# A mixer kernel's opening: inverse square root as a power on GpSimd, normalising on GpSimd, first weights from ScalarE's queue, more empty transposes

## The chip, the core and the metric

The kernel runs on one core of one Trainium2 chip. The core has TensorE (matrix products and transposes into PSUM), VectorE, ScalarE, GpSimd and a queue engine, SyncE, that issues most of the transfers. The metric is the time of one execution on the device in microseconds; less is better.

## What is computed

The input x has 2048 rows of 512 numbers. It is normalised along each row, and two branches work on the result: attention with 32 heads of 128 against a window of 512 keys, and a gated block that mixes along the rows. Cut to what matters:

```python
xn = layernorm(x)                                   # 2048 x 512, eps 1e-5
q = (xn @ wq) in 32 heads of 128
p = softmax(q @ k.T * 128**-0.5)                    # 512 keys for each head
s = (p @ v, heads side by side) @ wo
z = gelu(xn @ w_in)                                 # 1376 columns, in two halves of 688
z1, z2 = z[:, :688], layernorm(z[:, 688:])
g = silu((z1 * (w_sp @ z2 + b_sp)) @ w_out)
out = x + s * g
```

## The kernel before

Rows are cut into 16 tiles of 128. Every operand of a product is split into a rounded high part (by ScalarE, L165 and L208) and a low part, the rest (`rest`, L57); each product is three matmuls, high with high, low with high and high with low (`mm3`, L61 to L63). Each engine runs its instructions in the order in which the program writes them; the order is written out by hand, and transfers start in the order of their queue.

The kernel has three stages: attention together with the first half of the gated block's products, then the other half, then the mixing along the rows. This case is about the opening, the first 50 us of the first stage.

The opening brings each tile of x through these steps: load into `sacc` (L174), statistics (`ln_stats`: L181 and L183 on VectorE), inverse square root of the variance (`rsqrt_opening`, L116: one operation on VectorE, a square root on ScalarE, then a reciprocal and a correction in four operations on VectorE), normalising in place (`ln_apply`, L195, VectorE), four transposes on TensorE through PSUM (`ln_flip`, L206), cast to the high part (L208, ScalarE), rest to the low part (L57, VectorE). After that, the tile can go into products: `z1_piece`, twelve matmuls of 344 columns with the first quarter of w_in (the tiles `pT_h` and `pT_l`), whose result goes to memory from ScalarE's queue (L229); and `qproj`, the queries of one head for four tiles at a time.

The operations of an inverse square root are kept in a list, and `tick` puts one of them behind another instruction of VectorE; `finish` puts out what is left of a list before a tile is normalised. One root serves the tiles of one group (`GROUPS`): tiles 0 and 1 alone, 2 and 3 together, then four at a time.

Tiles 0 to 2 have their products in a prologue; each product is cut in the middle, and `start` puts the transposes of the next tile there. Then comes a loop over steps `t` from -7 on. Step `t` transposes tile `t + 11`, takes statistics and normalises for later tiles, makes one piece of the queries, and from `t = 0` on one score block (L259 and L261, softmax), from 12 on products with v, from 17 on the output projection. The list `Z0` says in which steps the products of tiles 3 to 15 with w_in are made.

At the very start TensorE has nothing to multiply, and 24 transposes of the identity into a PSUM tile that nobody reads (`warm`, L355) keep it occupied. SyncE's queue issues the loads in this order: tile 0 of x, first piece of w_in, tile 1, three pieces of w_in, tiles 2 and 3, first piece of the head's weights, tiles 4 to 7, three more pieces, and the rest of x.

Of the kernel before, what the change touches and what calls it, by code (L numbers as in the profile page):

```python
# [17 lines left out]
P = 128  # L18
S, D = 2048, 512
H, DH, W = 32, 128, 512  # L20
NT = S // P
NC = D // P
# [4 lines left out]
EPS = 1e-5  # L27
# [11 lines left out]
def mixer_kernel(ctx: ExitStack, tc: tile.TileContext, x, wh, w_in, w_sp, b_sp, w_out, out):  # L39
# [8 lines left out]
    nc = tc.nc  # L48
# [7 lines left out]
    def rest(engine, lo, whole, hi):  # L56
        engine.tensor_tensor(lo, whole, hi.bitcast(F32), op=OP.subtract)  # L57
# [10 lines left out]
    chains = []  # L68

    def tick(n=1):  # L70

        for _ in range(n):
            for c in list(chains):
                c.pop(0)()
                if not c:
                    chains.remove(c)

    def finish(chain):
        while chain:
            tick()  # L80
# [25 lines left out]
        nc.vector.memset(t[:, :4], 0.5)  # L106
        nc.vector.memset(t[:, 4:], float(0x5F3759DF - (1 << 22) - (1 << 31)))

    def rsqrt_opening(var, y, n, tmp, consts):

        v, r, a = ([tmp[:, k * n:k * n + n] for k in range(3)])
        chain = []
        chains.append(chain)

        def add(f, *args, **kw):
            chain.append(lambda: f(*args, **kw))  # L116

        add(nc.vector.scalar_tensor_tensor, v, var, EPS, consts[:, 8:8 + n], op0=OP.add, op1=OP.mult)
        add(nc.scalar.activation, r, v, AF.Sqrt, scale=-2.0)
        add(nc.vector.reciprocal, r, r)  # L120
        add(nc.vector.tensor_mul, a, r, r)
        add(nc.vector.tensor_mul, a, a, v)
        add(nc.vector.scalar_tensor_tensor, y, a, 1.5, r, op0=OP.add, op1=OP.mult)
        return chain

    stats = ctx.enter_context(tc.tile_pool(name="stats", bufs=2))
    left = ExitStack()
# [11 lines left out]
    sacc = sp.tile([P, NT, D], F32, name="sacc")  # L139
# [5 lines left out]
    def load_piece(key, k):  # L145
        n = 512 if key[0] == "h" else NB
        r = rawp.tile([P, 512], F32, name="raw")
        raw[key, k] = r
        nc.sync.dma_start(r[:, :n], (wh if key[0] == "h" else w_in)[key[1], :, k])

# [4 lines left out]
    def split_piece(key, k, engine):  # L155
        n = 512 if key[0] == "h" else NB
        if key == ("w", 0):
            hi = ap.tile([P, 512], F32R, name="pT_h", bufs=4)
            lo = ap.tile([P, 512], F32R, name="pT_l", bufs=4)
        else:  # L160
            f = FOLLOWS[key][k] if key in FOLLOWS else k
            hi = wp.tile([P, 512], F32R, name=f"wh{f}")
            lo = wp.tile([P, 512], F32R, name=f"wl{f}")
        r = raw.pop((key, k))[:, :n]
        nc.scalar.copy(hi[:, :n], r)  # L165
        rest(engine, lo[:, :n], r, hi[:, :n])
        wt[key, k] = (hi, lo)


    GROUPS = [(0, 1), (1, 2), (2, 4)] + [(a, a + 4) for a in range(4, NT, 4)]  # L170
    mv, rx, xT = {}, {}, {}

    def load_x(a, b):
        nc.sync.dma_start(sacc[:, a:b, :], x[a * P:b * P, :].rearrange("(g p) d -> p g d", p=P))  # L174

    def ln_stats(i):
        a, b = next(g for g in GROUPS if g[0] <= i < g[1])
        if i == a:
            mv[a] = stats.tile([P, 4, 2], F32, name="mv", bufs=4)
        stt = stats.tile([P, 6], F32, name="stt", bufs=4)  # L180
        nc.vector.bn_stats(stt, sacc[:, i, :])  # L181
        tick(2)
        nc.vector.bn_aggr(mv[a][:, i - a, :], stt)  # L183
        tick()
        if i == b - 1:
            r = stats.tile([P, 4], F32, name="rs_r", bufs=4)
            tmp = stats.tile([P, 12], F32, name="rs_t", bufs=3)
            chain = rsqrt_opening(mv[a][:, :b - a, 1], r[:, :b - a], b - a, tmp, consts)
            for j in range(a, b):
                rx[j] = mv[a][:, j - a, 0:1], r[:, j - a:j - a + 1], chain  # L190

    def ln_apply(i):
        mean, r, chain = rx[i]
        finish(chain)
        nc.vector.tensor_scalar(sacc[:, i, :], sacc[:, i, :], mean, r, op0=OP.subtract, op1=OP.mult)  # L195
        tick(2)

    def ln_flip(i):
        g, j = divmod(i, 4)
        if j == 0:  # L200
            hi = xp.tile([P, NC, 512], F32R, name="xh")
            lo = xp.tile([P, NC, 512], F32R, name="xl")
            xT[g] = (hi, lo)
        ps = ps_step.tile([P, NC, P], F32, name="ps_3")
        for c in range(NC):
            nc.tensor.transpose(ps[:, c, :], sacc[:, i, c * P:(c + 1) * P], ident)  # L206
        hi, lo = (t[:, :, j * P:(j + 1) * P] for t in xT[g])
        nc.scalar.copy(hi, ps)  # L208
        rest(nc.vector, lo, ps, hi)
        tick(2)  # L210


    def zmm(ps, i, n, cs):
# [17 lines left out]
    def z1_piece(i, n, between=lambda: None):  # L231
        z1_out(i, n, z1_product(i, n, between))
# [19 lines left out]
    def score(t):  # L252
        b, j = divmod(t, 4)
        ps = ps_step.tile([P, W], F32, name="ps_3")
        mm3(ps, True, True, cols(qT[b], j * P, (j + 1) * P), wt[("h", b // NQ), 1])
        if j == 0:
            sums[b] = ap.tile([P, 4], F32, name="sums", bufs=8)
        nm = ap.tile([P, 1], F32, name="nm", bufs=8)
        nc.vector.tensor_reduce(nm, ps, axis=AX.X, op=OP.max, negate=True)  # L259
        prob[t] = ap.tile([P, W], F32, name="prob", bufs=3)  # L260
        nc.scalar.activation(prob[t], ps, AF.Exp, bias=nm, accum_out=sums[b][:, j:j + 1])  # L261
# [20 lines left out]
    def shares(b, c):  # L282
        hi = ap.tile([P, 512], F32R, name="pT_h", bufs=4)
        lo = ap.tile([P, 512], F32R, name="pT_l", bufs=4)
        p, h, l = pL[b][:, :, Q * c:Q * c + Q], *(t.rearrange("p (i q) -> p i q", q=Q) for t in (hi, lo))
        nc.scalar.copy(h, p)  # L286
        rest(nc.vector if 4 * b + c >= NSTEP - 10 and c % 2 else nc.gpsimd, l, p, h)
        pT[b, c] = (hi, lo)
# [44 lines left out]
            plan(("w", 1 + n), k, NSTEP + d)  # L333

    load_x(0, 1)
    load_piece(("w", 0), 0)
    load_x(1, 2)
    for k in range(1, 4):
        load_piece(("w", 0), k)
    load_x(2, 4)  # L340
    load_piece(("h", 0), 0)
    load_x(4, 8)
    for k in range(1, 4):
# [3 lines left out]
    ident = const.tile([P, P], F32, name="ident")  # L347
    make_identity(nc, ident)
    consts = const.tile([P, 12], F32, name="consts")
# [1 line left out]
    nc.vector.memset(consts[:, 8:], -0.5)  # L351

    warm = ps_step.tile([P, NC, P], F32, name="ps_3")
    for k in range(24):
        nc.tensor.transpose(warm[:, k % NC, :], ident, ident)  # L355
    bsp = const.tile([P, NT], F32, name="bsp")
    nc.sync.dma_start(bsp, b_sp)

    ln_stats(0)
    ln_apply(0)  # L360
    ln_stats(1)
    for k in range(2):
        split_piece(("w", 0), k, nc.vector)
    ln_flip(0)
    for k in range(2, 4):
        split_piece(("w", 0), k, nc.vector)
    ln_apply(1)
    for i in (2, 3):
        ln_stats(i)

    def start(i):
        ln_flip(i + 1)
        for j in ((2, 3), (), (4, 5))[i]:
            ln_apply(j)
        for j in ((4, 5), (6, 7), (8, 9))[i]:
            ln_stats(j)
        tick((0, 11, 0)[i])

    for i in range(3):
        z1_piece(i, 0, lambda: start(i))  # L380
    split_piece(("h", 0), 0, nc.vector)

    Z0 = (-7, -6, -4, -3, -1, 0, 2, 4, 5, 6, 7, 8, 9)
    for t in range(T0, T1):
        for key in loads.get(t, ()):
            load_piece(*key)
        bq, cq = divmod(t + QL, 4)
        bm, cm = divmod(t - ML, 4)
        bp, cp = divmod(t - PL, 4)
        bo, jo = divmod(t - OL, 4)  # L390
        i = t + XL
        if i < NT:
            ln_flip(i)
        if 0 <= bm < NBLK:
            shares(bm, cm)
        for key, k in splits.get(t, ()):
            split_piece(key, k, nc.vector if t >= NSTEP - 4 and k % 2 else nc.gpsimd)
        if 0 <= t < NSTEP:
            score(t)
        if i + 6 < NT:  # L400
            ln_stats(i + 6)
        if i + 2 < NT:
            ln_apply(i + 2)
        if t in Z0:
            z1_piece(3 + Z0.index(t), 0)
        if 0 <= bq < NBLK:
            qproj(bq, cq)
        if 0 <= bp < NBLK:
            pv(bp, cp)
        if 0 <= bo < NBLK:  # L410
            outp(bo, jo)
        if 0 <= t - Z1 < NT - 1:
            ps = z1_product(t - Z1, 1)
        if 0 <= bq < NBLK:
            qproj_out(bq, cq)
        if 0 <= bp < NBLK:
            pv_out(bp, cp)
        if 0 <= t - Z1 < NT - 1:
            z1_out(t - Z1, 1, ps)
        if t % 4 == 2 and 0 <= t // 4 - 1 < NBLK:  # L420
            turned(t // 4 - 1)
        if 0 <= t - 1 < NSTEP:
            turn(t - 1)
# [283 lines left out]
```

## Time and profile before

| | |
|---|---|
| three runs | 1842.38, 1842.83, 1843.93 us |
| median | 1842.83 us |
| span of the profiled execution | 1839.7 us |
| TensorE busy in it | 1826.3 us |
| VectorE busy from 0 to 20 us | 14.46 us |
| TensorE busy from 0 to 20, 20 to 40 and 40 to 60 us | 14.64, 16.74 and 19.98 us |

The profiled execution is one execution with its own time, of which the span from the first to the last instruction is shown. In the lines, PE is TensorE, PEld its weight loads, DVE VectorE, ACT ScalarE, POOL GpSimd, SPq and ACTq the queues of SyncE and ScalarE. L206 is line 206 of the program. In the view by order of time the first two numbers are start and length in us, and a bracket at the end tells how long the engine was idle before the instruction and what ended that. Matmuls overlap in a pipeline, so the time from one start to the next says more than the length of one.

### The profile page before, as it was taken

The page shows a single profiled execution, that of the slowest core. Times are in us where ns is not written, and L with a number is a line of the kernel's source. Part 1 is how long each engine was busy: PE and PEld are TensorE (multiplying, and loading weights), DVE is VectorE, ACT ScalarE, POOL GpSimd, SP SyncE. Part 2 cuts the span into 40 slices and gives each one's busy share as a digit, 9 for nine tenths or more (in the row PEclk, how much of TensorE's full clock was granted, in tenths as well). Part 3 has the DMA queues.
Part 4 walks back from the last instruction along what each step waited for, and adds up shares of the span by engine and source line. Part 5 has one row for each costly group of instructions (what it writes and reads, how often), then busy time and mean ns, then how long its engine had stood idle before and what let it go on. Part 6 is the DMA issues. An engine that isn't in the chain of part 4 may idle for free.

```text
span 1839.7 us, 27536 instructions
## 1 busy us (share of the span) xinstructions
PE 1826.3 (99%) x8831; PEld 1572.6 (85%) x8831; DVE 1362.6 (74%) x2402; ACT 1020.1 (55%) x2190; POOL 851.4 (46%) x665
## 2 busy tenths in 40 slices
PE   8999999999999999999999999999999999999999
PEld 7888888888888888888888888888888999999998
DVE  7688888888888888888888888888888466333433
ACT  3566556666666656656666656656666445343422
POOL 0365555655665655555565556555656233000000
PEclk9999999999999999999999999999999999999999
DMA  4788888888888888888888888888888714554532
GB/s 166 193 231 218 218 220 219 218 215 223 214 218 217 218 218 215 213 221 216 220 221 215 221 226 213 221 215 217 216 220 223 223 59 153 174 184 140 180 122 91
DMA packets 404369, 368.99 MB, mean 201 GB/s; under 512 B 23072, under 2 KB 299296, under 8 KB 404224
## 3 DMA queue, kind: packets, MB, share of 16 engines
q1 hardware_dynamic: 399616, 361.59, 74.5%
q10 hardware_dynamic: 4608, 5.64, 0.9%
q8 instruction: 69, 1.13, 0.3%
q14 instruction: 76, 0.62, 0.1%
HBM read 213.00 MB, written 154.14 MB: 200 GB/s over the span
## 4 chain that ended last, share of the span: by engine, by line
PE 98%; DVE 0%; ACT 0%; issue 0%; DMA 0%; SPq 0%; ACTq 0%; DVEq 0%
PE ps_a L61 14%; PE ps_a L63 14%; PE ps_a L62 14%; PE ps L61 13%; PE ps L63 13%; PE ps L62 13%; PE ps_g L63 4%; PE ps_g L62 4%; PE ps_g L61 4%; PE ps_f L63 1%; PE ps_f L62 1%; PE ps_f L61 1%; PE ps L206 0%; PE ps_f L637 0%; DMA raw<-w_in 0%
## 5 line engine op out<-in xcount | busy, mean ns | idle before, releaser
L57 POOL TENSOR_TENSOR pT_l<-pL,pT_h 128x512 fp32r<-128x512 f32 x507 | 657.3, 1297 | 573.2 <-ACT pT_h L286 539.3
L261 ACT ACTIVATE prob<-ps,nm 128x512 f32<-128x512 f32 x512 | 353.2, 690 | 530.8 <-DVE nm L259 528.7
L313 DVE SCALAR_TENSOR_TENSOR sacc<-ps,sums,sacc 128x512 f32<-128x512 f32 x496 | 370.6, 748 | 173.2 <-PE ps L63 173.1
L269 DVE STREAM_TRANSPOSE pB<-prob 128x512 f32<-128x512 f32 x512 | 359.2, 702 | 1.4 <-DMA p_dram<-pB 0.9
L259 DVE TENSOR_REDUCE nm<-ps 128x1 f32<-128x512 f32 x512 | 334.8, 654 | 3.6 <-PE ps L63 3.6
L286 ACT CAST pT_h<-pL 128x512 fp32r<-128x512 f32 x512 | 315.9, 617 | 9.6 <-ACT z L228 4.2
L57 POOL TENSOR_TENSOR wl<-raw,wh 128x512 fp32r<-128x512 f32 (+1 forms) x132 | 169.5, 1285 | 81.2 <-ACT wh L165 81.2
L61 PE MATMUL ps<-wh,qT_h 128*128 128x512 f32 x512 | 199.9, 390 | 0.7 <-DVE sacc L311 0.7
L61 PE MATMUL ps_a<-xh,wh 128*128 128x512 f32 x512 | 199.4, 390 | 0.0
L62 PE MATMUL ps_a<-pT_l,wh 128*128 128x512 f32 x512 | 199.3, 389 | 0.0
L62 PE MATMUL ps_a<-xl,wh 128*128 128x512 f32 x512 | 199.3, 389 | 0.0
L62 PE MATMUL ps<-wl,qT_h 128*128 128x512 f32 x512 | 199.3, 389 | 0.0
L63 PE MATMUL ps<-wh,qT_l 128*128 128x512 f32 x512 | 199.2, 389 | 0.0
L63 PE MATMUL ps_a<-xh,wl 128*128 128x512 f32 x512 | 199.2, 389 | 0.0
L61 PE MATMUL ps_a<-pT_h,wh 128*128 128x512 f32 x512 | 199.2, 389 | 0.0
L61 PE MATMUL ps<-wh,oT_h 128*128 128x512 f32 x512 | 199.2, 389 | 0.0
L62 PE MATMUL ps<-wl,oT_h 128*128 128x512 f32 x512 | 199.2, 389 | 0.0
L63 PE MATMUL ps_a<-pT_h,wl 128*128 128x512 f32 x512 | 199.2, 389 | 0.0
L63 PE MATMUL ps<-wh,oT_l 128*128 128x512 f32 x512 | 199.2, 389 | 0.0
L63 PE MATMUL ps_g<-z_h,xl 128*128 128x344 f32 x512 | 161.8, 316 | 0.0
L61 PE MATMUL ps_g<-z_h,xh 128*128 128x344 f32 x512 | 161.8, 316 | 0.0
L62 PE MATMUL ps_g<-z_l,xh 128*128 128x344 f32 x512 | 161.8, 316 | 0.0
(133 smaller groups left out, 2981.5 us busy)
## 6 DMA issues: line engine op xcount, KB each, us to landing
p_dram<-pB SPq DMA_DIRECT2D x512, 256.0 KB, 3.5
pL<-p_dram SPq DMA_DIRECT2D x512, 256.0 KB, 5.6
raw<-wh SPq DMA_DIRECT2D x128, 256.0 KB, 4.4
xh<-w_sp SPq DMA_DIRECT2D x32, 256.0 KB, 5.7
xl<-w_sp SPq DMA_DIRECT2D x28, 256.0 KB, 5.8
u_dram<-uB SPq DMA_DIRECT2D x15, 384.0 KB, 2.3
uL<-u_dram SPq DMA_DIRECT2D x60, 96.0 KB, 2.1
z_dram<-z ACTq DMA_DIRECT2D x32, 172.0 KB, 2.3
```

Source lines behind the costliest of these rows:

```text
L57: engine.tensor_tensor(lo, whole, hi.bitcast(F32), op=OP.subtract)
L61: nc.tensor.matmul(ps, lh, rh, start=first, stop=False)
L62: nc.tensor.matmul(ps, lh, rl, start=False, stop=False)
L63: nc.tensor.matmul(ps, ll, rh, start=False, stop=last)
L259: nc.vector.tensor_reduce(nm, ps, axis=AX.X, op=OP.max, negate=True)
L261: nc.scalar.activation(prob[t], ps, AF.Exp, bias=nm, accum_out=sums[b][:, j:j + 1])
L269: nc.vector.transpose(pB.rearrange("p (k q) -> p k q", q=Q), prob.pop(t))
L286: nc.scalar.copy(h, p)
L313: nc.vector.scalar_tensor_tensor(sacc[:, i, :], ps, rs, sacc[:, i, :], op0=OP.mult, op1=OP.add)
```

## The change

- The inverse square root goes to GpSimd: an addition of the epsilon, then a power with exponent -0.5 (`consts` holds it in columns 8 to 11). The lists, `tick` and `finish` are no longer used in the opening.
- Groups have two tiles from tile 2 on (before: 2, then 4 each), and statistics in the loop are taken four tiles ahead instead of six.
- Tiles 0 and 1 are normalised on VectorE, tiles 2 to 15 on GpSimd.
- VectorE's order at the start is new: statistics of tiles 0 and 1, the split of the first piece of w_in, normalising of tiles 0 and 1, the rest for tile 0, the other three splits, statistics of tiles 2 and 3.
- The four first pieces of w_in are issued from ScalarE's queue, the loads of x follow one another on SyncE's.
- 29 empty transposes at the start instead of 24, and five more behind those of tile 0.
- `Z0` has other steps.

```diff
-    def rsqrt_opening(var, y, n, tmp, consts):
...
-        add(nc.vector.scalar_tensor_tensor, v, var, EPS, consts[:, 8:8 + n], op0=OP.add, op1=OP.mult)
-        add(nc.scalar.activation, r, v, AF.Sqrt, scale=-2.0)
-        add(nc.vector.reciprocal, r, r)
-        add(nc.vector.tensor_mul, a, r, r)
-        add(nc.vector.tensor_mul, a, a, v)
-        add(nc.vector.scalar_tensor_tensor, y, a, 1.5, r, op0=OP.add, op1=OP.mult)
-        return chain
+    def rsqrt_pool(var, y, n, v):
+        nc.gpsimd.tensor_scalar(v[:, :n], var, EPS, None, op0=OP.add)
+        nc.gpsimd.tensor_tensor(y[:, :n], v[:, :n], consts[:, 8:8 + n], op=OP.pow)
...
-        nc.sync.dma_start(r[:, :n], (wh if key[0] == "h" else w_in)[key[1], :, k])
+        queue = nc.scalar if key == ("w", 0) else nc.sync
+        queue.dma_start(r[:, :n], (wh if key[0] == "h" else w_in)[key[1], :, k])
...
-    GROUPS = [(0, 1), (1, 2), (2, 4)] + [(a, a + 4) for a in range(4, NT, 4)]
+    GROUPS = [(0, 1), (1, 2)] + [(a, a + 2) for a in range(2, NT, 2)]
...
-            chain = rsqrt_opening(mv[a][:, :b - a, 1], r[:, :b - a], b - a, tmp, consts)
+            rsqrt_pool(mv[a][:, :b - a, 1], r, b - a, stats.tile([P, 2], F32, name="rs_t", bufs=4))
...
+    def ln_apply(i, engine):
+        mean, r = rx[i]
+        engine.tensor_scalar(sacc[:, i, :], sacc[:, i, :], mean, r, op0=OP.subtract, op1=OP.mult)
...
     load_x(0, 1)
-    load_piece(("w", 0), 0)
+    for k in range(4):
+        load_piece(("w", 0), k)
     load_x(1, 2)
-    for k in range(1, 4):
-        load_piece(("w", 0), k)
...
-    for k in range(24):
-        nc.tensor.transpose(warm[:, k % NC, :], ident, ident)
+    def fill(n):
+        for k in range(n):
+            nc.tensor.transpose(warm[:, k % NC, :], ident, ident)
+    fill(29)
...
     ln_stats(0)
-    ln_apply(0)
     ln_stats(1)
-    for k in range(2):
+    split_piece(("w", 0), 0, nc.vector)
+    ln_apply(0, nc.vector)
+    ln_apply(1, nc.vector)
+    ln_flip(0)
+    fill(5)
+    for k in range(1, 4):
         split_piece(("w", 0), k, nc.vector)
-    ln_flip(0)
-    for k in range(2, 4):
-        split_piece(("w", 0), k, nc.vector)
-    ln_apply(1)
     for i in (2, 3):
         ln_stats(i)
 
     def start(i):
         ln_flip(i + 1)
-        for j in ((2, 3), (), (4, 5))[i]:
-            ln_apply(j)
-        for j in ((4, 5), (6, 7), (8, 9))[i]:
+        for j in ((2, 3), (4,), (5,))[i]:
+            ln_apply(j, nc.gpsimd)
+        for j in ((4, 5), (6, 7), ())[i]:
             ln_stats(j)
-        tick((0, 11, 0)[i])
...
-    Z0 = (-7, -6, -4, -3, -1, 0, 2, 4, 5, 6, 7, 8, 9)
+    Z0 = (-7, -6, -5, -4, -3, -2, -1, 0, 1, 2, 4, 7, 9)
...
-        if i + 6 < NT:
-            ln_stats(i + 6)
+        if i + 4 < NT:
+            ln_stats(i + 4)
         if i + 2 < NT:
-            ln_apply(i + 2)
+            ln_apply(i + 2, nc.gpsimd)
```

More of the change, by code (lines that the diff above doesn't have):

```diff
@@ L107, in set_consts @@
         nc.vector.memset(t[:, 4:], float(0x5F3759DF - (1 << 22) - (1 << 31)))
-    def rsqrt_opening(var, y, n, tmp, consts):
[L111 to L116, printed above, removed]
-        add(nc.vector.scalar_tensor_tensor, v, var, EPS, consts[:, 8:8 + n], op0=OP.add, op1=OP.mult)
-        add(nc.scalar.activation, r, v, AF.Sqrt, scale=-2.0)
-        add(nc.vector.reciprocal, r, r)
-        add(nc.vector.tensor_mul, a, r, r)
-        add(nc.vector.tensor_mul, a, a, v)
-        add(nc.vector.scalar_tensor_tensor, y, a, 1.5, r, op0=OP.add, op1=OP.mult)
-        return chain
+    def rsqrt_pool(var, y, n, v):
+        nc.gpsimd.tensor_scalar(v[:, :n], var, EPS, None, op0=OP.add)
+        nc.gpsimd.tensor_tensor(y[:, :n], v[:, :n], consts[:, 8:8 + n], op=OP.pow)
     stats = ctx.enter_context(tc.tile_pool(name="stats", bufs=2))
@@ L178, in ln_stats @@
         if i == a:
-            mv[a] = stats.tile([P, 4, 2], F32, name="mv", bufs=4)
+            mv[a] = stats.tile([P, 2, 2], F32, name="mv", bufs=5)
         stt = stats.tile([P, 6], F32, name="stt", bufs=4)
         nc.vector.bn_stats(stt, sacc[:, i, :])
-        tick(2)
         nc.vector.bn_aggr(mv[a][:, i - a, :], stt)
-        tick()
         if i == b - 1:
-            r = stats.tile([P, 4], F32, name="rs_r", bufs=4)
-            tmp = stats.tile([P, 12], F32, name="rs_t", bufs=3)
-            chain = rsqrt_opening(mv[a][:, :b - a, 1], r[:, :b - a], b - a, tmp, consts)
+            r = stats.tile([P, 2], F32, name="rs_r", bufs=5)
+            rsqrt_pool(mv[a][:, :b - a, 1], r, b - a, stats.tile([P, 2], F32, name="rs_t", bufs=4))
             for j in range(a, b):
[L190 to L196, printed above, removed]
+                rx[j] = mv[a][:, j - a, 0:1], r[:, j - a:j - a + 1]
+    def ln_apply(i, engine):
+        mean, r = rx[i]
+        engine.tensor_scalar(sacc[:, i, :], sacc[:, i, :], mean, r, op0=OP.subtract, op1=OP.mult)
     def ln_flip(i):
@@ L209, in ln_flip @@
         rest(nc.vector, lo, ps, hi)
-        tick(2)
     def zmm(ps, i, n, cs):
```

## The prediction

> **What bounds the kernel now.** I read the page first, then TensorE's waits in the first 60 us, then the granted clock in stretches, then the opening in order of time.
>
> ```profile
> span 1839.7 us, 27536 instructions
> PE 1826.3 (99%) x8831; PEld 1572.6 (85%) x8831; DVE 1362.6 (74%) x2402; ACT 1020.1 (55%) x2190; POOL 851.4 (46%) x665
> ```
>
> TensorE is busy for all but 13.4 us. The change touches none of its products, so it can only win idle time and slow-clock time. The waits of TensorE from 0 to 60 us (total, times, longest) show where most of it lies:
>
> ```profile
> PE ps L206 <- DVE sacc L195: 2.7, 2, 2.0
> PE ps L206 <- issue: 2.3, 1, 2.3
> PE ps L355 <- POOL ident masks.py:199: 1.4, 1, 1.4
> PE ps L61 <- ACT xh L208: 1.2, 1, 1.2
> PE ps L206 <- ACT qT_h L248: 1.0, 1, 1.0
> ```
>
> These make 8.6 us, nearly all in front of L206, the transposes of a normalised tile. The columns of the next view are stretch, length, busy time of PE, PEld, DVE, ACT and POOL, the granted clock, DMA share and GB/s:
>
> ```profile
> 4.10:7.50 3.40, 2.06 (x17) 1.58 (x15) 2.74 (x11) 1.06 (x4) 0.00 (x0) 1.00 0.98 276
> 7.50:10.90 3.40, 1.48 (x6) 0.90 (x6) 2.63 (x9) 1.43 (x4) 0.00 (x0) 1.00 1.00 302
> 10.90:14.30 3.40, 2.66 (x11) 2.66 (x12) 2.95 (x8) 0.68 (x2) 0.00 (x0) 0.50 1.05 404
> 14.30:17.70 3.40, 3.40 (x14) 3.31 (x14) 3.05 (x10) 1.14 (x3) 0.00 (x0) 0.50 1.05 387
> ```
>
> After a stretch with TensorE 44% busy the clock is 0.50 for 6.8 us; 2.66 + 3.40 = 6.06 us of work run there at half pace, so about 3.0 us are lost. After the stretch with 61% it stayed at 1.00. Idle time and clock together put about 11.6 us in reach, part of it the unavoidable arrival of data. The order of time (start, length):
>
> ```profile
> 0.73 0.37 SPq L174 DMA_DIRECT2D sacc<-x  x1
> 0.73 1.28 ACT L116 ACT_TABLE_LOAD   x1 [0.73 <-PEq L699]
> 1.63 0.42 SPq L174 DMA_DIRECT2D sacc<-x  x1
> 3.41 0.69 DVE L181 BATCH_NORM_STATS2 stt<-sacc 128x6 f32<-128x512 f32 x1 [2.38 <-DMA sacc<-x]
> 4.51 0.43 SPq L174 DMA_DIRECT2D sacc<-x  x1
> 5.57 0.55 DVE L195 TENSOR_SCALAR sacc<-sacc,mv,rs_r 128x512 f32<-128x512 f32 x1
> 6.17 0.66 PE L206 MATMUL ps<-ident,sacc 128*128 128x128 f32 x4 [0.67 <-DVE sacc L195]
> 6.85 0.50 DVE L57 TENSOR_TENSOR pT_l<-raw,pT_h 128x344 fp32r<-128x344 f32 x1
> 8.01 0.69 DVE L57 TENSOR_TENSOR xl<-ps,xh 128x512 fp32r<-128x512 f32 x1
> 11.50 0.69 DVE L181 BATCH_NORM_STATS2 stt<-sacc 128x6 f32<-128x512 f32 x1
> 11.64 1.11 PE L206 MATMUL ps<-ident,sacc 128*128 128x128 f32 x4 [1.99 <-DVE sacc L195]
> 12.32 0.66 DVE L181 BATCH_NORM_STATS2 stt<-sacc 128x6 f32<-128x512 f32 x1
> 14.99 0.34 ACTq L229 DMA_DIRECT2D z_dram<-z  x1
> 23.06 0.63 PE L206 MATMUL ps<-ident,sacc 128*128 128x128 f32 x4 [2.30 <-issue]
> 23.73 0.59 ACT L208 CAST xh<-ps 128x512 fp32r<-128x512 f32 x1 [0.58 <-PE ps L206]
> ```
>
> Tiles 0, 1 and 4 are transposed at 6.17, 11.64 and 23.06; the last two had to wait for VectorE, which does statistics, root chain, normalising and both splits in one queue. My landmark is the transposes of tile 4: in both kernels TensorE has by then done tiles 0 to 3 and three products, and nothing else that counts.
>
> **The change, part by part.** Prices first: the pitch of products and GpSimd's groups (line, operation, count | busy us, mean ns | idle).
>
> ```profile
> 24.00 0.32 PE L61 MATMUL ps<-pT_h,xh 128*128 128x344 f32 x1
> ...
> 24.79 0.32 PE L63 MATMUL ps<-pT_h,xl 128*128 128x344 f32 x1
> ```
> ```profile
> L57 POOL TENSOR_TENSOR pT_l<-pL,pT_h 128x512 fp32r<-128x512 f32 x507 | 657.3, 1297 | 573.2 <-ACT pT_h L286 539.3 <-DMA raw<-wh 12.4 <-DMA p_dram<-pB 10.1
> L57 POOL TENSOR_TENSOR wl<-raw,wh 128x344 fp32r<-128x344 f32 x5 | 4.8, 956 | 14.0 <-ACT wh L165 14.0
> masks.py:199 POOL TENSOR_SCALAR_AFFINE_SELECT ident<-ident 128x128 f32<-128x128 f32 x1 | 0.3, 292 | 0.1
> L699 POOL MEMSET const-float32-0.0<- 128x1 f32 x1 | 0.1, 98 | 0.2 <-issue 0.2
> ```
>
> Five product starts in 0.79 us: 0.158 each, so twelve (one tile) take 1.9 us. *Power on GpSimd*: an add, about 0.1 us (as the memset), and a power of one or two elements, which no row shows. The two TENSOR_TENSOR rows differ by 0.34 us for 168 columns, which leaves 0.26 us for none; ends 0.1 (memset) and 1.3 us (a full 512 columns). I take 0.5: nearest to 0.26, with something for a harder function. With three hand-overs of 0.1 us (an estimate) a root takes about 0.9 us. *Normalising on GpSimd*: from 98 ns for one column and 292 for 128, 512 columns make 0.87 us; ends 0.55 (VectorE's own) and 1.3. *Removed*: per group five small operations of VectorE and one of ScalarE, and from tile 2 on VectorE's normalising; ScalarE's root also needed a table of its own, so the load before the exponentials goes too (I count nothing for it: TensorE waited for no table).
>
> *Weights on ScalarE's queue*: four issues at 0.34 us push the table load of 1.28 us to about 2.1 to 3.4, before any weight can have landed, so it costs nothing; if the weights came first, up to 0.7 us. SP's queue is three issues shorter ahead of tile 1. Its load of tiles 4 to 7 now waits until the first weight piece has landed, at about the 4.51 of before; later loads of h0 still wait for the splits that free their buffers.
>
> ```profile
> sacc<-x SPq DMA_DIRECT2D x2, 256.0 KB, 3.1
> sacc<-x SPq DMA_DIRECT2D x3, 1024.0 KB, 9.6
> ```
>
> Tile 0 took 2.7 us (0.73 to 3.41); with a median of 3.1 tile 1 took 3.5 and was there at 5.1. It is now issued 0.5 us earlier (4.6), but a further 172 KB of weights from the other queue runs beside it (0.6 us at 276 GB/s: 5.7). I take 5.4. VectorE now takes the statistics of tile 1 ahead of normalising tile 0, so this landing is on the path. Statistics are 0.82 us apart (11.50, 12.32), the split takes 0.5, and 0.6 lie between the start of normalising and the transposes (5.57, 6.17): tile 0 is transposed at 5.4 + 0.82 + 0.5 + 0.6 = 7.3, 1.1 us later than before.
>
> From there: transposes and cast 1.3, split 0.69 (VectorE free at 9.3), three weight splits 1.5, statistics of tiles 2 and 3 1.64: 12.4; split of tile 1 0.69: 13.1. Tile 1 itself is normalised at 7.8 and no longer waits, so the first product is done by then, and the second can use its low part from 13.1. Root 0.8 and normalising 0.87 on GpSimd after 12.4: tile 2 is transposed at 14.15, and six products more end at 14.15 + 0.63 + 0.95 = 15.7. Tiles 4 to 7 land by 4.51 + 9.6 = 14.1; two statistics: 15.75; split of tile 2: 16.45. Ten of the third product's twelve and tile 3's transposes: 1.6 + 0.63. **Tile 4 at 18.7 instead of 23.06: 4.4 us won.** Later steps need 1.5 of VectorE (0.69 + 0.82) and about 1.3 of GpSimd per tile, below TensorE's 1.9 + 0.63, so the 1.0 us wait at L248, where the transposes were held by a late normalising, goes as well.
>
> *Products moved to other steps*: steps -5, -2 and 1 get one, 5, 6 and 8 lose one.
>
> ```profile
> L269 DVE STREAM_TRANSPOSE pB<-prob 128x512 f32<-128x512 f32 x512 | 359.2, 702 | 1.4 <-DMA p_dram<-pB 0.9
> L259 DVE TENSOR_REDUCE nm<-ps 128x1 f32<-128x512 f32 x512 | 334.8, 654 | 3.6 <-PE ps L63 3.6
> ```
>
> A step without one has six products of 512 columns, 6 x 0.235 (0.158 scaled by 512/344) = 1.41 us, against 1.36 of VectorE: covered, narrowly; if not, some 0.2 us in each of three steps. *Empty transposes*: ten.
>
> ```profile
> 1.60:2.00 0.40, 0.40 (x3) 0.40 (x3) 1.00 0.64 159
> 4.40:4.80 0.40, 0.40 (x7) 0.40 (x5) 1.00 0.85 184
> ```
>
> These are the empty transposes alone: 3 touch a stretch of 0.4 us early, 7 at 4.4, so they doubled their pace with nothing else on TensorE. The fill of before ended at 5.5 (6.17 less its 0.67 of idle); five more, at no more than the 0.63 of four, end by 6.3, before 7.3, and the five behind tile 0 lie in the wait for its cast; neither delays anything at full clock. The Trainium skill, TensorE: Matmul & The Clock Gate, Part 4 (PE-mode transpose), says the opposite: transposes don't bring the full clock. By that rule the fill is worthless and TensorE would open at half pace, which is the first rival below; the trace disagrees for these transposes (3 against 7).
>
> The sum: 1839.7 - 4.4 - 1.0 = 1834.3 us of span. The runs' median of 1842.83 lies 3.1 above the profiled span, so 1837.4.
>
> **The rivals.** *The clock falls all the same.* With my times TensorE does in 7.5 to 10.9 us some 0.4 of transposes, 0.55 of fill, 0.95 of products and 0.63 of tile 1, 2.5 us; in 10.9 to 14.3 it is 0.95 + 0.3 + 0.63 = 1.9, or 55%, between the 44% that lost the clock and the 61% that kept it. Half pace costs up to the 3.0 of before, less what hides in VectorE's waits; I take 2.5: 1839.9.
>
> *The power is slow.* The power has TensorE behind it twice in each group: in GpSimd's queue it stands ahead of the next normalising, and from VectorE's queue the splits wait behind normalising tile 1. With P us for a power, P = 4 (three full TENSOR_TENSORs) has tile 0 ready at 9.2, tile 1 at about 13, statistics of tiles 2 and 3 at 16.8, tile 2 at 22, tile 4 at about 28: 5 us later than before, less the 1.0: 1847, and some 9 us more at P = 5, since a pair of tiles then takes 5.3 + 1.7 on GpSimd. It loses from about P = 3 on. No row of GpSimd comes near that for so few elements; against it, no row shows a power.
>
> *A first use stalls GpSimd.* If the first power takes X us longer once, tile 0 has 1.7 us of room (root at 5.0, needed at 6.7) and everything moves by the rest; 5.4 + 1.7 = 7.1 is the point of no gain.
>
> ```profile
> 31.55 1.29 POOL L57 TENSOR_TENSOR wl<-raw,wh 128x512 fp32r<-128x512 f32 x1 [30.25 <-ACT wh L165]
> 31.79 1.07 DVE L116 TENSOR_TENSOR rs_t<-rs_t 128x4 f32<-128x4 f32 x1
> ```
>
> GpSimd's first TENSOR_TENSOR took 1.29 against a mean of 1.297, so X was 0 there; an X of half the room lost, 3.5 us beyond it, gives 1840.9. The Trainium skill, GPSIMD Engine Reference, section 2.1, gives about 6 us for the first call of a freshly loaded kernel; by that figure 1841.7.
>
> *VectorE is held while GpSimd works.* The second row is a product of four columns that took 1.07 us beside that TENSOR_TENSOR. If the statistics of three tiles are each held for one normalising, 3 x 0.87 = 2.6 are lost: 1840.0. *Nothing changes*, because another wait stands behind each: 1842.8.
>
> **How the numbers follow.** Forecast 0.50, clock 0.23, slow power 0.14, first use 0.05, VectorE held 0.05, nothing 0.03. Measurement tells 0.2%, 3.7 us, from no change: faster is below 1839.1, slower above 1846.5. Faster: the forecast and a third of the clock case, 0.58. Slower: most of the slow power, 0.13. Same: 0.29. The forecast alone runs from 1836.0 (landing at 4.6, no hold by tiles 4 to 7) to 1839.0 (landing at 5.7, power 1.3, three uncovered steps); the range goes on through the clock, first-use and unchanged cases to 1843.5, and at the low end to 1835.3 if normalising takes VectorE's 0.55.
>
> **What would show it.** Transposes of tiles 0, 1, 2 and 4 near 7.3, 9.7, 14.2 and 18.7; a power of at most 1.3 us; clock 1.00 throughout; no wait at L248's place; no new wait in steps 3 to 12. Wrong it is if a power or its first use takes several us, if the clock falls at 9 to 15 us, or if tile 1 lands after 6.

## The result, and the profile after

The changed kernel takes 1846.28 us (median of 16 runs, 1843.89 to 1848.81), the kernel before 1842.96 beside it (16 runs, 1841.13 to 1843.93): the ratio is 1.0022 with a 95% interval of 1.0015 to 1.0029. By the medians it is slower by 3.3 us, where 1837.4 was forecast and the range ended at 1843.5. The profiled execution has a span of 1845.5 us, 5.8 more than the one of before; it is the run of 1847.57 us, 1.3 above the median, so the 5.8 that is taken apart below is more than the median's loss. Of the 16 runs the eight with a mean clock of 0.998 or 0.999 took 1843.9 to 1846.2 us, the eight with 0.995 to 0.997 took 1846.4 to 1848.8.

The page's first lines and TensorE's longest waits over the whole span of the changed kernel (total, times, longest in us):

```profile
span 1845.5 us, 27554 instructions
PE 1832.0 (99%) x8841; PEld 1577.5 (85%) x8841; DVE 1351.2 (73%) x2358; ACT 1017.5 (55%) x2183; POOL 888.3 (48%) x697
```
```profile
PE ps_g L61 <- DVE rz_r L92: 3.2, 1, 3.2
PE ps L190 <- POOL sacc L180: 1.9, 1, 1.9
PE ps L339 <- POOL ident masks.py:199: 1.4, 1, 1.4
PE ps_a L61 <- ACT pT_h L269: 1.0, 1, 1.0
PE ps L63 <- DVE xl L57: 0.9, 1, 0.9
PE ps_a L62 <- POOL pT_l L57: 0.8, 1, 0.8
```

L180 is the normalising, L190 the transposes, L339 the empty transposes, L269 the cast of the softmax's probabilities. The wait at the place of L248 is gone. The longest wait, the first row, lies in no stage that the change touches: `ps_g` is the mixing along the rows, 1536 us into the span. The transposes of the tiles in the opening, in order of time:

```profile
7.02 0.60 PE L190 MATMUL ps<-ident,sacc 128*128 128x128 f32 x4
9.86 0.60 PE L190 MATMUL ps<-ident,sacc 128*128 128x128 f32 x4
15.34 0.66 PE L190 MATMUL ps<-ident,sacc 128*128 128x128 f32 x4 [1.85 <-POOL sacc L180]
18.71 1.06 PE L190 MATMUL ps<-ident,sacc 128*128 128x128 f32 x4
20.73 0.60 PE L190 MATMUL ps<-ident,sacc 128*128 128x128 f32 x4
```

The last row is tile 4, the landmark of the prediction: 20.73 instead of 23.06, so 2.3 us are won there, and TensorE is idle for 0.05 us from 20 to 40 us (busy 19.95; 16.74 before). Up to 60 us the kernel is ahead. Three stretches of the changed kernel tell the rest (stretch, length, busy time of PE, PEld, DVE, ACT and POOL with instruction counts, granted clock, DMA share, GB/s):

```profile
10.90:14.30 3.40, 1.72 (x10) 1.12 (x8) 3.11 (x9) 0.63 (x2) 2.06 (x3) 1.00 1.05 394
14.30:17.70 3.40, 2.36 (x13) 2.17 (x14) 1.05 (x2) 1.03 (x2) 3.32 (x4) 0.84 1.05 396
17.70:21.10 3.40, 3.40 (x19) 3.34 (x18) 1.86 (x5) 0.75 (x2) 3.21 (x4) 0.66 0.76 265
80.00:84.00 4.00, 2.45 (x10) 1.47 (x8) 1.18 (x2) 1.70 (x4) 1.00 (x1) 1.00 0.96 336
84.00:88.00 4.00, 3.69 (x10) 2.92 (x11) 2.00 (x4) 2.41 (x6) 2.79 (x3) 0.61 0.79 170
1535.00:1540.00 5.00, 1.94 (x13) 1.66 (x11) 3.21 (x17) 1.30 (x3) 2.66 (x2) 0.90 0.86 265
1540.00:1545.00 5.00, 4.86 (x17) 4.86 (x18) 3.88 (x7) 4.08 (x7) 1.67 (x1) 0.50 0.80 294
1545.00:1550.00 5.00, 5.00 (x31) 5.00 (x30) 4.00 (x7) 4.00 (x8) 0.52 (x1) 0.92 0.64 189
```

First, the clock falls in the opening (0.84, 0.66) behind the wait for tile 2. Second, from 80 to 88 us TensorE is idle for 1.9 us and its clock is 0.61 in the second half; before, it was busy in all of these 8 us, at 1.00. Third, from 1535 to 1545 it is idle for 3.2 us and then at 0.50; before, the same stretches were full:

```profile
1535.00:1540.00 5.00, 5.00 (x35) 5.00 (x34) 3.35 (x14) 1.89 (x4) 2.92 (x2) 1.00 0.71 207
1540.00:1545.00 5.00, 5.00 (x34) 5.00 (x34) 3.71 (x10) 3.03 (x5) 2.10 (x2) 1.00 0.95 337
```

Two landmarks split the 5.8 us of span, the first `ps_g` product and the first of the final projection (`ps_f`), of the changed kernel and of the one before:

```profile
1536.32 0.32 PE L61 MATMUL ps_g<-z_h,xh 128*128 128x344 f32 x1
...
1572.60 0.40 PE L61 MATMUL ps_f<-wo_h,xh 128*128 128x512 f32 x1
```
```profile
1537.36 0.32 PE L61 MATMUL ps_g<-z_h,xh 128*128 128x344 f32 x1
...
1566.80 0.39 PE L61 MATMUL ps_f<-wo_h,xh 128*128 128x512 f32 x1
```

At the first the changed kernel is 1.04 ahead, at the second 5.80 behind. So all of the loss, 6.8 us, falls into 36 us of a stage whose code is the same in both kernels. Of the 6.8, the wait is 3.2. The shares 0.90, 0.50 and 0.92 make 6.8 us at half pace, of which 5.7 lie behind the wait and cost 2.8. The last 0.8 is a slower pace of the products behind the wait: at a clock of 1.00, three start in 0.47 us, where before three start in 0.46 (192 products in 29.44 us). What sets that pace is not shown.

What differs there is an address. The inverse square roots of the second stage (L92, VectorE) use a scratch tile `tmps` in PSUM, from the same four banks (4 to 7) as the opening's `ps_3` tiles. Later `ps_g1` takes banks 4 and 5 and `ps_f` 6 and 7. A tile's bank is fixed when the program is built, and the built programs list it: in the one of before the scratch lies in bank 6, in the changed one in bank 4. With bank 4, the fourth of the `ps_g` products, the first into `ps_g1`, must wait until the last root chain has left the scratch. The rows (start, length) show it: the chain's last operation starts at 1539.93, the product follows.

```profile
1539.93 0.16 DVE L92 SCALAR_TENSOR_TENSOR rz_r<-ps,rz_h 128x2 f32<-128x2 f32 x1
1540.14 0.66 PE L61 MATMUL ps_g<-z_h,xh 128*128 128x344 f32 x1 [3.20 <-DVE rz_r L92]
```

In the kernel before the same chain ended at 1541.1, but it stood in the bank of `ps_f`, which was needed at 1566.8 only. The sequence of banks in the two programs parts at the seventh `ps_3` tile, in the opening, and stays parted.

### The profile page after: what moved, and what is told of

Read it like the earlier page. It is cut to its first block, busy times and chain, and to the rows that moved or that the text cites. A ratio compares the mean times of both kernels' runs of the same rounds, so it can differ in the third digit from the quotient of the medians.

```text
span 1845.5 us, 27554 instructions
## 1 busy us (share of the span) xinstructions
PE 1832.0 (99%) x8841; PEld 1577.5 (85%) x8841; DVE 1351.2 (73%) x2358; ACT 1017.5 (55%) x2183; POOL 888.3 (48%) x697
## 4 chain that ended last, share of the span: by engine, by line
PE 97%; DMA 1%; DVE 1%; ACT 1%; POOL 1%; issue 0%; ACTq 0%; SPq 0%; DVEq 0%; POOLq 0%
PE ps_a L62 14%; PE ps_a L63 14%; PE ps_a L61 14%; PE ps L63 13%; PE ps L61 13%; PE ps L62 13%; PE ps_g L61 4%; PE ps_g L62 4%; PE ps_g L63 4%; PE ps_f L62 1%; PE ps_f L61 1%; PE ps_f L63 1%; DMA raw<-w_in 0%; PE ps_f L622 0%; DMA pL<-p_dram 0%; PE ps L190 0%
## 5 line engine op out<-in xcount | busy, mean ns | idle before, releaser
L269 ACT CAST pT_h<-pL 128x512 fp32r<-128x512 f32 x512 | 316.0, 617 | 10.2 <-DMA pL<-p_dram 4.5
```

## The experiments

Each was timed beside the kernel before (1843.66, 1843.29 and 1842.88 us in the three sets); differences are against that. The intervals of the ratios are about 0.001 to each side, 2 us, so differences below that are not told from nothing, unless the text says that ranges don't overlap.

### The bank of the scratch

Two kernels move the scratch alone, with throw-away tiles ahead of it (one small VectorE memset each): the changed kernel with bank 6, and the kernel before with bank 4.

```diff
+    for _ in range(2):      # changed kernel: bank 4 -> 6; in the kernel before range(1): bank 6 -> 4
+        nc.vector.memset(ps_step.tile([P, 512], F32, name="ps_3")[:, :8], 0.0)
     tmps = ps_step.tile([P, 512], F32, name="ps_3")
```

> The changed kernel with two more tiles taken from the pool of the PSUM tile ps_3 just ahead of the scratch tile tmps, so that the scratch of the second stage's root chain lies in bank 6, as it did in the kernel before, and not in bank 4, the first bank of the third stage's ps_g1. Theory 1, the scratch's bank is what the change lost: the wait of 3.2 us of ps_g for the root chain goes, and with it the slow clock behind it (0.85 over 20 us, 3.0 us of work): 1846.3 - 6.2 = 1840.1, faster than before by 2 to 4 us. Theory 2, the loss is in the opening and the steps behind it and the wait at the third stage only shows it late: the wait moves elsewhere and the time stays within 1.5 us of 1846.3.

> The kernel before with one more ps_3 tile taken ahead of tmps, which puts the scratch in bank 4; nothing else is changed. Theory 1: the same wait appears at the start of the third stage, some 3.5 us and 3 us of slow clock: 1849.2. Theory 2: no wait, 1843.

Changed kernel with bank 6: 1840.66 us, ratio 0.9983 [0.9974, 0.9992], 3.0 faster than before. The wait of `ps_g` is gone, TensorE is busy from 1535 to 1550 at a clock of 1.00, and the other waits of the list stay. Kernel before with bank 4: 1848.40 us, 1.0028 [1.0017, 1.0039], 4.7 slower, and it has the row of the changed kernel, which its own profile lacked:

```profile
PE ps_g L61 <- DVE rz_r L92: 3.2, 1, 3.2
```

The bank alone, moved in both directions, is worth 4.7 us on the kernel before and 6.3 on the changed one (+3.3 against -3.0). A part of that is the clock. In the profiled execution of the kernel before with bank 4, the quickest of its seven runs, the clock stays at 1.00 behind the wait, and from the first `ps_g` to the first `ps_f` product it takes 33.75 us (1537.61 to 1571.36), 4.3 more than the 29.44 of before; the changed kernel took 36.28. Of the kernels of this document only these two, the changed one and the one before with bank 4, have the wait; in all others the scratch lies in bank 6 or 7. With the bank out of the way the change is a gain.

### Normalising on GpSimd, and the moved products

Both start from the changed kernel with bank 6. One takes the old steps `Z0`, the other normalises all tiles on VectorE.

```diff
-    Z0 = (-7, -6, -5, -4, -3, -2, -1, 0, 1, 2, 4, 7, 9)
+    Z0 = (-7, -6, -4, -3, -1, 0, 2, 4, 5, 6, 7, 8, 9)
```
```diff
-            ln_apply(j, nc.gpsimd)
+            ln_apply(j, nc.vector)
...
-            ln_apply(i + 2, nc.gpsimd)
+            ln_apply(i + 2, nc.vector)
```

> The changed kernel with the scratch in bank 6 and the steps of Z0 of the kernel before. Theory Z, the moved products laid bare the way of the probabilities through memory: the two waits of 1.0 and 0.8 us at 82 to 84 us and the slow clock behind them (1.8 us) go, while the steps without a product at -5 and -2 now wait for GpSimd (4.2 us for two tiles): 1839 to 1840, with the waits at other places. Theory G, those waits come from GpSimd or the loads and not from Z0: they stay, and GpSimd's are added: 1842 or more.

> The changed kernel with the scratch in bank 6 and all tiles normalised on VectorE, the root still on GpSimd. If GpSimd's 2.08 us for a tile is what costs at tile 2 (1.85 us of wait and the slow clock behind it), tile 2 is transposed some 1.2 us earlier and the time is 1 to 2 us below that of the same kernel with normalising on GpSimd: about 1838.5. If VectorE's queue, which then waits for each root, gives it back: 1840 to 1842.

Old steps: 1843.57, ratio 1.0003 [0.9994, 1.0012], so 2.9 of gain lost. Neither expectation gave that: of the two waits at 82 to 84 us the longer went, but the waits for GpSimd cost more than the 4.2 put down for them. All on VectorE: 1838.56, 0.9975 [0.9965, 0.9985], 2.1 better than with GpSimd; the runs (1838.07 to 1839.31) don't overlap those of the kernel with GpSimd (1839.35 to 1841.17). The groups of GpSimd in the changed kernel, and VectorE's one in the same trace, show why (count | busy us, mean ns):

```profile
L180 POOL TENSOR_SCALAR sacc<-sacc,mv,rs_r 128x512 f32<-128x512 f32 x14 | 29.0, 2081 | 0.2
L112 POOL TENSOR_TENSOR rs_r<-rs_t,consts 128x2 f32<-128x2 f32 x7 | 5.0, 716 | 0.6
L112 POOL TENSOR_TENSOR rs_r<-rs_t,consts 128x1 f32<-128x1 f32 x2 | 1.3, 649 | 0.2
```
```profile
L180 DVE TENSOR_SCALAR sacc<-sacc,mv,rs_r 128x512 f32<-128x512 f32 x2 | 1.1, 542 | 0.5 <-POOL rs_r L112 0.5
```

Normalising takes 2.08 us on GpSimd, 3.8 times VectorE's 0.54. With an addition and half a power of two columns, GpSimd needs about 2.6 us per tile, as much as TensorE's 1.9 + 0.63. In steps with no product with w_in to fill the time, TensorE then waits; with the old steps the wait is six times there:

```profile
PE ps L190 <- POOL sacc L180: 6.9, 6, 1.9
```

So the new `Z0`, with products in every step from -7 to 2, hides GpSimd's slowness: it belongs to the normalising, not to the root. This trace also tells what held tile 4 in the changed kernel. Its clock is 1.00 throughout the opening, and tile 4 still comes no sooner than at 20.84, from GpSimd; in the changed kernel GpSimd ended the normalising of tile 4 at 20.55. The rows are of the changed kernel, then of the one with the old steps:

```profile
18.46 2.09 POOL L180 TENSOR_SCALAR sacc<-sacc,mv,rs_r 128x512 f32<-128x512 f32 x1
```
```profile
20.84 0.66 PE L190 MATMUL ps<-ident,sacc 128*128 128x128 f32 x4 [0.93 <-POOL sacc L180]
```

So the low clock behind tile 2 delayed tile 4 by 0.2 us at most.

The new `Z0` has its own price, seen from 80 to 88 us in the changed kernel (start, length):

```profile
82.30 0.62 ACT L269 CAST pT_h<-pL 128x512 fp32r<-128x512 f32 x1 [3.02 <-DMA pL<-p_dram]
82.97 0.51 PE L61 MATMUL ps_a<-pT_h,wh 128*128 128x512 f32 x1 [1.03 <-ACT pT_h L269]
84.31 0.50 PE L62 MATMUL ps_a<-pT_l,wh 128*128 128x512 f32 x1 [0.84 <-POOL pT_l L57]
```

With no product with w_in in steps 5 and 6, the softmax blocks of steps 5 to 8 come close together: their exponentials start at 62.79, 64.50, 65.17 and 66.72, where those of before took from 61.54 to 68.38. Their probabilities go through memory at nearly the same time, and the transfers take longer. The rows are of the kernel before and of the changed one, from 55 to 90 us (issues, KB each, median us to landing):

```profile
p_dram<-pB SPq DMA_DIRECT2D x13, 256.0 KB, 3.5
```
```profile
p_dram<-pB SPq DMA_DIRECT2D x13, 256.0 KB, 5.5
```

ScalarE then waited 3.02 us for the load of the probabilities, and the products behind it waited as well. In every kernel of this document with the new list this median is 5.3 to 5.7 us, in every one with the old list 3.5 to 4.0, and 4.1 with the list between them that follows.

The next two keep VectorE for normalising and take the old `Z0`, and one between old and new.

```diff
+    Z0 = (-7, -6, -4, -3, -1, 0, 2, 4, 5, 6, 7, 8, 9)      # old
+    Z0 = (-7, -6, -5, -4, -3, -1, 0, 2, 4, 6, 7, 8, 9)     # between
```

> The changed kernel with the scratch in bank 6, all tiles normalised on VectorE, and the steps of Z0 of the kernel before; to be held against the same with the new steps, 1838.56. Theory L: products moved ahead of step 0 push the first scores back, while the products with v come sooner, so the way of the probabilities through memory is laid bare at 80 to 84 us (2.2 us of wait, 1.8 us of slow clock); with the old steps these go, and steps -5 and -2 without a product wait for VectorE, some 0.9 us each (2.05 us a tile against 1.14): 1836 to 1837. Theory D: the loads of that stretch are the limit whatever the order of the products, the waits stay and VectorE's are added: 1839 to 1841.

> The same kernel with steps between the two lists (-7, -6, -5, -4, -3, -1, 0, 2, 4, 6, 7, 8, 9: seven products from step 0 on, the new list has six, the old one eight). Theory L: about half of the waits at 80 to 84 us go and one early step waits: 1836.5 to 1837.5. Theory D: 1838.5 to 1840.

Old steps: 1837.74, ratio 0.9970 [0.9958, 0.9981], the lowest median of all. TensorE's wait for the cast of the probabilities (1.4 us with the new list) is gone, the clock is 1.00 in every stretch from 7.5 to 100 us, tile 4 is transposed at 18.32, and the first `ps_g` product starts at 1532.87, 4.5 ahead of before. Between: 1838.71, 0.9976 [0.9966, 0.9986]. The three lists can't be told apart by time (1838.56, 1837.74, 1838.71) when VectorE normalises, though their waits differ; with GpSimd the choice was worth 2.9. The time of the old steps lies between the ranges of theories L and D and that of the list between in the range of D, while the waits went as theory L says; time does not decide between the two.

### The root alone, and the empty transposes

The first is the kernel before with nothing changed but the root (groups, order, queue and `Z0` as before; the scratch lies in bank 7). The second is the changed kernel with VectorE normalising, with 24 empty transposes and none behind tile 0.

```diff
-        add(nc.vector.scalar_tensor_tensor, v, var, EPS, consts[:, 8:8 + n], op0=OP.add, op1=OP.mult)
...
-        add(nc.vector.scalar_tensor_tensor, y, a, 1.5, r, op0=OP.add, op1=OP.mult)
+        chains.remove(chain)
+        nc.gpsimd.tensor_scalar(v, var, EPS, None, op0=OP.add)
+        nc.gpsimd.tensor_tensor(y, v, consts[:, 8:8 + n], op=OP.pow)
```
```diff
-    fill(29)
+    fill(24)
...
-    fill(5)
```

> The kernel before with the root alone made by GpSimd (an addition and a power for a group, groups of up to four, orders, loads, fill and steps of before; the scratch lies in bank 7). If the five small operations and the way over ScalarE are what holds tile 1 and tile 4 back, tile 1 is transposed near 9.5 instead of 11.6 and tile 4 near 21 instead of 23.1, and the time falls by 2 to 3 us to about 1841. If the order of VectorE's queue holds them, tile 1 gains (its root no longer stands behind two splits) but tile 4 little: 1842.5 to 1843.5.

> The changed kernel with the scratch in bank 6, all tiles normalised on VectorE, and the empty transposes of the kernel before: 24 at the start, none behind tile 0; against 1838.56. If the empty transposes hold the clock, TensorE is busy for about 2.5 of the 4 us from 4 to 8 instead of 3.6, the clock falls to 0.5 near 9 to 11 us for one or two stretches of 3.4 us, and the time is 1840 to 1841.5. If the products alone hold it: 1838.5.

Root alone: 1838.53, ratio 0.9972 [0.9961, 0.9983], 4.8 faster. Tile 4 comes at 19.57, TensorE has no idle time from 20 to 60 us and keeps a clock of 1.00. This one part is nearly all of what was won in any version, and more than the 2 to 3 us that were expected of it.

Fewer empty transposes: 1838.02, 0.9972 [0.9961, 0.9983], against 1838.56 with them. The clock does fall without them. The rows are of the kernel with 34 empty transposes, then of the one with 24, from 4.1 to 14.3 us:

```profile
4.10:7.50 3.40, 3.02 (x24) 2.78 (x23) 2.75 (x7) 0.48 (x1) 1.96 (x4) 1.00 1.04 339
7.50:10.90 3.40, 3.13 (x21) 2.46 (x19) 3.02 (x8) 2.34 (x5) 0.00 (x0) 1.00 0.98 355
10.90:14.30 3.40, 2.40 (x15) 1.81 (x14) 2.79 (x7) 0.62 (x3) 0.94 (x2) 1.00 1.02 365
```
```profile
4.10:7.50 3.40, 2.45 (x17) 2.10 (x15) 2.64 (x7) 0.48 (x1) 1.95 (x4) 1.00 1.03 332
7.50:10.90 3.40, 2.73 (x11) 2.12 (x10) 3.02 (x7) 1.82 (x4) 0.00 (x0) 0.65 1.01 353
10.90:14.30 3.40, 3.40 (x21) 3.05 (x19) 2.91 (x7) 1.03 (x2) 0.94 (x2) 0.84 1.05 392
```

At 0.65 and 0.84 TensorE only fills time in which it otherwise waited for the next tile: tile 4 is transposed at 18.39 against 18.28. The empty transposes hold the clock, and the clock is worth nothing there that could be measured. By the Trainium skill, TensorE: Matmul & The Clock Gate, Part 4 (PE-mode transpose), transposes don't bring the full clock; these two traces, which differ in ten transposes, disagree.

### Tiles 2 and 3 alone

The changed kernel with only tiles 2 and 3 normalised on VectorE. No tile is added: with this the scratch lies in bank 7 by itself, which ties its place in bank 4 to these two tiles.

```diff
-            ln_apply(j, nc.gpsimd)
+            ln_apply(j, nc.vector if j < 4 else nc.gpsimd)
```

> The changed kernel with tiles 2 and 3 alone normalised on VectorE; tiles 4 to 15 stay on GpSimd and no scratch tile is added. With these two tiles the order in which PSUM tiles come free stays such that the scratch of the third stage lies in a bank of its own (7). Theory (the changed kernel loses 5.6 us to the bank and 2.1 us to GpSimd's normalising, most of that at tile 2): no wait of the first ps_g on rz_r, tile 2 transposed near 13.5, about 1839 to 1840. Rival (normalising on GpSimd loses in the loop too): about 1841, as with all of tiles 2 to 15 on GpSimd and the scratch out of the way.

1839.51, ratio 0.9981 [0.9972, 0.999], 3.4 faster than before and 6.7 below the changed kernel, by one line of its text. There is no wait of `ps_g`, tile 2 is transposed at 13.64. Whether tiles 4 to 15 on GpSimd cost the 1.0 us that still lies above all on VectorE can't be told at 2 us. The two small waits that they leave:

```profile
PE ps L190 <- POOL sacc L180: 0.8, 2, 0.5
```

### The queue of the first weights, and the plainest version

The first is the best version with the first pieces of w_in on SyncE's queue again, in the order of before; the second has 24 empty transposes as well.

```diff
-        queue = nc.scalar if key == ("w", 0) else nc.sync
+        queue = nc.sync
...
     load_x(0, 1)
-    for k in range(4):
-        load_piece(("w", 0), k)
+    load_piece(("w", 0), 0)
     load_x(1, 2)
+    for k in range(1, 4):
+        load_piece(("w", 0), k)
```

> The fastest version so far (root on GpSimd, all tiles normalised on VectorE, old steps Z0, scratch in bank 6, 1837.74 us) with the four first pieces of w_in issued from SyncE's queue again, in the order of before. If the queue of these pieces is immaterial: the same to 0.7 us. If the earlier pieces pay or the later landing of x costs: tile 0 lands near 3.4 instead of 4.1 and the time moves by about 1 us in the one or the other direction.

> As the run before it, and with 24 empty transposes and none behind tile 0: of the change only the root on GpSimd, groups of two and the new order of VectorE at the start are left. If empty transposes and the clock of the opening are worth nothing, 1837.7 as the version with them; if they are worth what the clock loses in the opening (up to 3 us), up to 1840.

1838.63, ratio 0.9976 [0.9967, 0.9986], and 1838.32, 0.9972 [0.9961, 0.9984]: 4.3 and 4.6 faster than before, not to be told from the best version's 5.6. The loads do move: tile 0's statistics begin at 3.38 and 3.50 instead of 4.01, but tile 1's at 5.84 and 5.59 instead of 5.07. VectorE takes them ahead of normalising tile 0, so tile 0 is transposed at 7.69 and 7.44 instead of 6.92. Queue and empty transposes, by these runs, are worth less than 2 us. The second pair of traces repeats what the empty transposes do: from 7.5 to 10.9 and from 10.9 to 14.3 us the clock is 1.00 with 34 of them, 0.71 and 0.79 with 24.

### What makes GpSimd's normalising slow

This kernel, with the scratch in bank 6, leaves out part of the normalising of nine tiles, so that four forms of the operation stand side by side in one trace.

```diff
-        engine.tensor_scalar(sacc[:, i, :], sacc[:, i, :], mean, r, op0=OP.subtract, op1=OP.mult)
+        if i < 4 or i % 4 == 0:
+            engine.tensor_scalar(sacc[:, i, :], sacc[:, i, :], mean, r, op0=OP.subtract, op1=OP.mult)
+        elif i % 4 == 1:
+            engine.tensor_scalar(sacc[:, i, :], sacc[:, i, :], 0.01, 20.0, op0=OP.subtract, op1=OP.mult)
+        elif i % 4 == 2:
+            engine.tensor_scalar(sacc[:, i, :], sacc[:, i, :], mean, None, op0=OP.subtract)
+        else:
+            engine.tensor_scalar(sacc[:, i, :], sacc[:, i, :], 20.0, None, op0=OP.mult)
```

> The changed kernel with the scratch in bank 6, in which GpSimd's normalising of tiles 4 to 15 has other forms, to price the operation; the normalising of these tiles is in part left out. Tiles 4, 8, 12 as they are (two operations, each with a number per partition), 5, 9, 13 two operations with constants, 6, 10, 14 one subtraction of a number per partition, 7, 11, 15 one multiplication by a constant. If it is the number per partition that makes it slow: 2.1, then near 0.9, then 1.5, then below 0.9 us. If it is the count of operations: 2.1, 2.1, 1.05, 1.05. If GpSimd takes about 2 us for any pass of this kind over 512 columns: 2.1 in all four.

GpSimd's groups in that trace, four forms and the two-input TENSOR_TENSOR of the same size:

```profile
L57 POOL TENSOR_TENSOR wl<-raw,wh 128x512 fp32r<-128x512 f32 x127 | 164.6, 1296 | 14.1 <-DMA p_dram<-pB 12.2 <-ACT wh L154 1.8
L181 POOL TENSOR_SCALAR sacc<-sacc,mv,rs_r 128x512 f32<-128x512 f32 x5 | 10.4, 2085 | 0.3
L183 POOL TENSOR_SCALAR sacc<-sacc 128x512 f32<-128x512 f32 x3 | 5.8, 1935 | 0.2
L185 POOL TENSOR_SCALAR sacc<-sacc,mv 128x512 f32<-128x512 f32 x3 | 4.7, 1567 | 0.3
L187 POOL TENSOR_SCALAR sacc<-sacc 128x512 f32<-128x512 f32 x3 | 4.5, 1502 | 0.2
```

None of the three guesses holds. A pass of one operation takes 1.50, the second operation 0.43 more, and a number per partition instead of a constant 0.07 each. Even the simplest pass is slower than the difference of two inputs at 1.30. The kernel was timed once, at 1839.32, 1.3 below the same kernel with all of the normalising: one run, so what the cheaper forms are worth is not shown.

## Why the prediction was wrong

**The sum** is the step that failed: "The sum: 1839.7 - 4.4 - 1.0 = 1834.3 us of span". It has no term for any stage behind the opening; the reason stands at its start: "The change touches none of its products, so it can only win idle time and slow-clock time." The code of the third stage is the same, but the change alters which PSUM tiles come free in which order, and so the bank of a tile 1500 us later, and that made a new wait. It is worth +6.3 on the changed kernel, shown both ways. No case of the range held it; the only rival that came near, a slow power at 1847, would have been near for a wrong reason. Of the 11.2 us between 1834.3 and the measured span of 1845.5, 6.8 lie in the 36 us at 1540, 2.0 in tile 4, and the other 2.3 between the two, where the waits of 1.9 us at 82 us and the half pace behind them lie.

Taken apart in four steps, against the kernel before: the root alone gives -4.8; everything else of the change with VectorE normalising -0.3 more, within what can be measured; GpSimd normalising +2.1 (with the old steps it would be 5.5); the bank +6.3. Together +3.3.

**Normalising at 0.87 us** was mis-sized: 2.08, beyond the upper end of 1.3. The price was drawn from a memset and a mask row, of which neither has two operations. Tile 2 came at 15.34 instead of 14.15, which is the difference of one normalising (2.08 - 0.87 = 1.21). Tile 4 came at 20.73 instead of 18.7: GpSimd had tiles 2 and 3, a root and tile 4 to do one after the other and ended at 20.55, where the prediction had GpSimd in the way of tile 2 only and let tile 4 hang on VectorE and TensorE. With VectorE normalising, tile 4 came at 18.28 and the kernel at 1838.56, near the 18.7 and 1837.4 of the prediction. "Later steps need ... about 1.3 of GpSimd per tile" falls with it, 2.6 being as much as TensorE has.

**"covered, narrowly; if not, some 0.2 us in each of three steps"**, the moved products: wrong in place. The steps that lost a product didn't wait. The products that read their probabilities some 20 us later did, 1.9 us and then about 3 us at half pace, because softmax blocks bunched and their transfers took longer. Its price can't be told by time with VectorE normalising.

**Right were**: the power (0.65 for one column, 0.72 for two, against 0.5, with no slow first use: the first took 0.58; the addition ahead of it took 0.23 to 0.41 against 0.1), tiles 0 and 1 (7.02 and 9.86 against 7.3 and 9.7), tile 1's landing (5.1 at the latest against 5.4), and the wait at L248's place. That the opening is held by the root's small operations was right too: the root alone brought tile 4 from 23.06 to 19.57. The 5.4 us of the sum are near the 5.6 of the best version, but that is in part luck: this version normalises on VectorE and has the old `Z0`, which is not the kernel that was priced. One reading was too strong: of the 8.6 us of waits at the start, 6.0 stand in front of L206, not nearly all.

**The rivals**: the clock fell, as the first of them said, though only behind 14.3 us, and the 2.5 us it was priced at were not there: tile 4 waited for GpSimd anyway, and the fall without empty transposes cost nothing that could be measured. VectorE was not held: its statistics took 681 ns on average, 679 before.

## What to carry to other kernels

A change in one place can move the addresses of tiles far away: where a rotating pool serves several stages, list the banks of both programs, and look for a wait on a tile that no changed line names. Price an operation by a row with the same count of operations on the same engine; GpSimd took 3.8 times VectorE's time for the same normalising, so the engine that had room was not the better place. Take the parts of a change apart before judging it: here one part was worth 4.8 us, another cost 2.1, an accident cost 6.3, and the rest could not be measured.

## What the runs showed of the hardware

- GpSimd's pass over 128x512 with one operation took 1.50 to 1.57 us, with two 1.94 to 2.08; a two-input TENSOR_TENSOR took 1.30. The Trainium skill, GPSIMD Engine Reference, section 4.1, calls GpSimd "roughly line-rate" for one input and about half as fast for two; here one input was the slower.
- A power on GpSimd took 0.65, 0.72 and 1.04 us for one, two and four columns, so the first column costs the most.
- The same wait of 3.20 us was followed by 5.7 us at half clock in the changed kernel and left the clock at 1.00 in the kernel before with bank 4. The rows of the latter:

```profile
1535.00:1540.00 5.00, 3.23 (x22) 2.96 (x20) 3.38 (x13) 2.13 (x4) 2.68 (x2) 1.00 0.70 206
1540.00:1545.00 5.00, 3.57 (x22) 3.57 (x23) 3.68 (x12) 2.79 (x5) 2.30 (x2) 1.00 0.93 333
```

There the wait ended at 1541.43, in the changed kernel at 1540.14. These are two single executions, and the clock differs between executions of one program: the changed kernel's runs with a mean clock of 0.999 have room for 5.5 us at half clock at most (0.0015 x 1844 us x 2, with rounding), so not all of them lost it as long as this one. What decides it was not tried.
- The clock also fell around a shorter wait: with 1.85 us in front of tile 2's transposes, TensorE busy for 1.72 and 2.36 of 3.40 us in the two stretches that hold it, the clock of the changed kernel was 0.84 in the second of them and 0.66 in the next.
